# A new work order for a one-core attention and convolution kernel: sines first, fewer filter transfers

## The chip, the cores and the metric

The kernel runs on one core of one Trainium2 chip. The metric is the device time of one execution in microseconds (us). The kernel before took 321.59 us as the median of three runs (320.0, 321.59 and 323.23).

The engines, with the names that the profile gives them: PE is TensorE (matmuls; PEld its weight loads), DVE is VectorE, ACT is ScalarE, POOL is GpSimd, SP is SyncE, which here only issues DMAs. POOL issues DMAs too.

## What is computed

Two layers. The first is linear attention with exponential features, for 8 batches, 8 heads, 576 positions and heads of 64; the second is a gated convolution over the 576 positions, with a circular convolution that the reference does by an FFT:

```python
def phi(x):
    proj = np.einsum('bhsd,df->bhsf', x, w_phi)
    proj = proj - np.max(np.abs(proj), axis=-1, keepdims=True)
    return np.concatenate([np.exp(proj), np.exp(-proj)], axis=-1)
q_p, k_p = (phi(q), phi(k))
kv = np.einsum('bhsf,bhsd->bhfd', k_p, v)
z = np.sum(k_p, axis=2)
num = np.einsum('bhsf,bhfd->bhsd', q_p, kv)
den = np.einsum('bhsf,bhf->bhs', q_p, z)[..., None] + 1e-06
x = (num / den).transpose(0, 2, 1, 3).reshape(8, 576, 512)
...
proj = x @ w_proj
x1, x2, x3 = proj[..., :D], proj[..., D:2 * D], proj[..., 2 * D:]
X2 = np.fft.rfft(x2, n=S, axis=1)
H = np.fft.rfft(filter_fft, n=S, axis=0)[None, :, :]
y = x1 * np.fft.irfft(X2 * H, n=S, axis=1) * x3
return y @ w_out
```

Inputs and output are float32; the kernel multiplies in bfloat16 and accumulates in float32. w_phi is 64 by 128, w_proj 512 by 1536, the filter 576 by 512, w_out 512 by 512, the output 8 by 576 by 512.

## The kernel before

The work is cut into steps, one small method each, and the order of all steps is written out by hand as one long string, `PLAN`. A word of it is a step with its arguments; DVE, ACT or POOL among the arguments picks the engine that does it, and `@n` picks the PSUM bank (of eight) where it starts. `run` reads the words one after the other and emits their instructions. So each engine, and each engine's own list of DMA issues, does its instructions in the order of the words; between engines only data and buffers decide, through semaphores. A step that waits holds up everything behind it on its engine.

The rows of `seq` are taken modulo 9, so that 576 positions are 64 groups of 9, and the two halves X (heads 0 to 3 and 4 to 7) are loaded together. b is the batch, v one of four pairs of heads (v of 0 and 1 in half X = 0, of 2 and 3 in X = 1), m one of four column blocks.

Steps that the change and the prediction touch:

- Loads: `loadh,k,0,X` and `loadh,q,0,X` (L581) load a half of batch 0, `load,n,b` (L575) a whole q, k or v, `w_load,proj,kt` (L565) a third of w_proj (the parts of x1, x2, x3), `w_load,out` w_out. POOL issues these, with a cast to bfloat16. `filt_load` (L496) and `filt_loadt` (L500) load the filter, SP issues these.
- Transposes: batch 0's q and k go through PE (`pt`, L597) and are copied out by `pte` (L286 or L284); from batch 1 on `trh,n,b,X` (L587) does it as a DMA transpose of half X, issued by SP. The attention's output x is transposed by `ptx` on PE in batch 0, with `ptxe` copying it out, and by `trx` and `trxt` as DMA transposes later.
- Tables of the convolution's transform: `gen_part`, `gen_ident`, `gen_rows`, `gen_back` on POOL, `gen_cols` and `gen_angles` on DVE, and `gen_sin` (L456, twelve sines in four calls) on ACT. `D1m` and `D1e` mirror one of them, `gen_five` (L477 to L490) copies the ends of some into M5, `gen_neg` and `gen_ends` make variants for the last batch. The filter is folded by `filt_fold` (L508) and transformed by five `H` (L526), emptied by `H_ev`.
- Attention: `Pk`, `Qn` (L616, L623) and their rests `Pkt`, `Qnt` are the projections, `maxk`, `maxq` (L692) their maxima, `ex`, `exkt`, `exqt` (L678, L681, L686) the exponentials, `em` those of the maxima. `mhi`, `mlo`, `trm`, `trme` bring q's maxima to the other side, `Pq` (L650) projects q once more with them taken off. `vs` scales v, `KV` (L754) and `KVe` make the sums, `NE` (L768), `rc`, `xn` the quotient.
- Convolution: `f1` (L836), `f2` (L842) fold x, `F` (L848, L852) transforms it, `Fe`, `Fet` empty it, `X1`, `X2`, `X3` (L892, L870) project, `X1e`, `tm` form the gate, `Y1` (L880) multiplies by the filter, `m3` (L884) adds two parts, `I` (L945) transforms back, `Ie`, `Ip`, `Im` and `ym` (L993) finish; batch 7 uses `J` (L983) and `yj` (L987) for this. `O` (L1004) is the last product, `Oe` empties it, `st` stores it (two DMAs of 128 KB each). `yt` moves a rest of yT.

ACT computes a sine or an exponential with a table that must be loaded when the function changes (ACT_TABLE_LOAD in the trace); copies need none. The compiler puts these loads in.

Some pairs of DVE and POOL steps are kept apart: `port` lets a POOL step of the kinds in `PORT` wait for the last such DVE step (or `gen_angles`, `yt`) before it in the string.

The loop that makes the program out of the string:

```python
for word in PLAN.split():
    name, _, bank = word.partition("@")
```

## Time and profile before

| | us |
|---|---|
| median of three runs | 321.59 |
| the profiled execution | 316.38 |
| its span, first to last instruction | 314.6 |
| PE busy | 275.2 (87%) |
| DVE busy | 263.1 (84%) |
| ACT busy | 220.8 (70%) |
| POOL busy | 215.6 (69%) |
| granted TensorE clock, mean | 0.991 |

The profile is of one execution. A window has its busy times for each engine; a group is a line with its operation, its tiles, the count and the duration of one; the chain of waits goes back from the last instruction to what released each step. "issue" in it is time in which an engine waited for nothing that the profile shows. A busy share of 100% doesn't mean that PE gives all that it could, since matmuls overlap and their ends are modelled. The larger DMA groups of the opening: sixteen filter transfers of 64 KB with a median of 5.3 us from issue to landing, k and q of a batch (576 KB) with 8.3 and 10.1 us, a third of w_proj (512 KB) with 17.9 us.

### The profile page before, as it was taken

To read this page: it belongs to the slowest core of one execution; us is meant where nothing else is said; L and a number is where in the kernel's file an instruction comes from. 1 tells how busy PE (TensorE), PEld (TensorE's weight loads), DVE (VectorE), ACT (ScalarE), POOL (GpSimd) and SP (SyncE) were. 2 spreads that over 40 slices of the span, in tenths; PEclk is the share of its full clock that TensorE was granted. 3 is DMA by queue.
4 is the path that set the end of the run, shared out by engine and by line. 5 is a ranking of instruction groups with operands and counts; after the bars stand their busy time and mean duration, and the time that the engine had idled before them with its cause. 6 is when DMAs were issued, how large, how long until landed. Compare 5 with 4: busy or idle time off the path is not lost.

```text
span 314.6 us, 10164 instructions
## 1 busy us (share of the span) xinstructions
PE 275.2 (87%) x4266; PEld 200.3 (64%) x4289; DVE 263.1 (84%) x466; ACT 220.8 (70%) x369; POOL 215.6 (69%) x183
## 2 busy tenths in 40 slices
PE   1366668999899999999998979999999999999981
PEld 1233357767687777687666747786678676867750
DVE  8498769999989999979996898989999968883940
...
GB/s 127 225 210 178 197 180 172 117 185 85 128 124 176 193 150 103 176 186 117 131 184 115 136 123 51 75 115 145 165 48 19 147 114 70 3 58 154 36 9 158
DMA packets 72030, 39.98 MB, mean 127 GB/s; under 512 B 52336, under 2 KB 66800, under 8 KB 71984
## 3 DMA queue, kind: packets, MB, share of 16 engines
...
## 4 chain that ended last, share of the span: by engine, by line
PE 69%; DVE 11%; issue 6%; DMA 5%; ACT 4%; POOL 2%; SPq 0%; ACTq 0%; DVEq 0%; POOLq 0%
PE ps L892 16%; PE ps L870 10%; PE ps L1004 9%; PE ps L754 5%; PE ps L945 5%; PE ps L768 4%; DVE mq L692 3%; PE ps L848 3%; PE ps L852 2%; DMA fl<-in_moe_filter_fft_dram 2%; DMA flt<-in_moe_filter_fft_dram 2%; PE ps L901 2%; PE ps L650 2%; PE ps L656 2%; PE ps L616 2%
## 5 line engine op out<-in xcount | busy, mean ns | idle before, releaser
L892 PE MATMUL ps<-xT,wproj 128*128 128x256 bf16 x512 | 63.4, 273 | 0.0
L892 PEld LDWEIGHTS <-wproj 128*128 128x128 bf16 x512 | 48.3, 98 | 8.7
L692 DVE TENSOR_REDUCE mq<-ps 128x8 f32<-128x1024 f32 (+1 forms) x40 | 43.6, 1110 | 3.4 <-PE ps L623 2.9
L993 POOL TENSOR_TENSOR yT<-cv,x1s 128x576 bf16<-128x576 f32 x28 | 35.3, 1279 | 15.8 <-DVE cv L952 12.7
L692 DVE TENSOR_REDUCE mk<-ps 128x8 f32<-128x1024 f32 (+1 forms) x40 | 44.0, 1109 | 0.1
L836 POOL TENSOR_TENSOR SD<-xn 128x512 bf16<-128x512 bf16 x25 | 28.4, 1153 | 21.6 <-DVE xn L787 18.1
L678 ACT ACTIVATE Eqp<-ps 128x1024 bf16<-128x1024 f32 x32 | 32.6, 1025 | 10.5 <-PE ps L656 8.9
L739 POOL TENSOR_TENSOR vm<-vn,vm 128x1152 bf16<-128x1152 bf16 x16 | 34.4, 2151 | 7.7 <-ACT vm L733 4.5
L678 ACT ACTIVATE Ekm<-ps 128x1024 bf16<-128x1024 f32 x32 | 32.7, 1029 | 6.4 <-DVE mk L692 3.7
L842 POOL TENSOR_TENSOR xf<-SD 128x512 bf16<-128x512 bf16 x30 | 34.0, 1153 | 3.4 <-DVE xf L842 1.9
L1004 PE MATMUL ps<-wout,yT 128*128 128x512 bf16 x134 | 33.6, 379 | 2.2 <-DVE yT L987 0.8
L739 POOL TENSOR_TENSOR vp<-vn,vp 128x1152 bf16<-128x1152 bf16 x16 | 34.4, 2150 | 1.6 <-ACT vp L733 1.6
L678 ACT ACTIVATE Eqm<-ps 128x1024 bf16<-128x1024 f32 x32 | 32.7, 1028 | 2.5 <-PE ps L656 2.4
L678 ACT ACTIVATE Ekp<-ps 128x1024 bf16<-128x1024 f32 x32 | 32.9, 1032 | 1.4 <-PE ps L616 1.3
L870 PE MATMUL ps<-wproj,XF 128*128 128x512 bf16 x119 | 29.9, 380 | 0.8 <-issue 0.5
L945 PE MATMUL ps<-inv,T 128*128 128x288 bf16 x168 | 23.2, 286 | 0.2 <-DVE mq L692 0.2
L952 DVE TENSOR_TENSOR cv<-es,ps 128x288 f32<-128x288 f32 x56 | 22.1, 445 | 1.5 <-ACT es L949 1.3
L949 ACT COPY es<-ps 128x288 f32<-128x288 f32 x28 | 11.0, 402 | 17.2 <-PE ps L945 17.2
L1004 PEld LDWEIGHTS <-yT 128*128 128x128 bf16 x144 | 13.1, 97 | 15.5 <-issue 2.0
L933 DVE TENSOR_TENSOR x1s<-ps,x1s 128x512 bf16<-128x512 f32 x32 | 21.5, 683 | 1.3 <-PE ps L892 1.0
L787 DVE TENSOR_TENSOR xn<-ps,r 128x512 bf16<-128x512 f32 x32 | 21.7, 685 | 0.8
L284 ACT CAST x1s<-ps 128x512 bf16<-128x512 f32 (+1 forms) x27 | 14.1, 533 | 11.1 <-PE ps L892 8.3
...
## 6 DMA issues: line engine op xcount, KB each, us to landing
...
qn<-in_q_dram POOLq DMA_DIRECT2D x7, 576.0 KB, 10.1
...
wproj<-in_moe_w_proj_dram POOLq DMA_DIRECT2D x3, 512.0 KB, 17.9
...
```

Source lines behind the costliest of these rows:

```text
L678: self.nc.scalar.activation(e, p, AF.Exp, bias=0.0, scale=1.0 if g == "p" else -1.0)
L692: self.nc.vector.tensor_reduce(out=out, in_=src, axis=AX.X, op=ALU.max, apply_absolute_value=True)
L739: self.eng(eng).tensor_tensor(out=t[:, :, :, 0:64], in0=self.at("vn", b)[:, 2 * X:2 * X + 2], in1=t[:, :, :, 64:65].to_broadcast([128, 2, ...
L787: self.nc.vector.tensor_tensor(out=o, in0=n[:, :, :, 0:64], in1=self.at("r", 4 * b + v).to_broadcast([128, 2, 4, 64]), op=ALU.mult)
L836: self.eng(eng).tensor_tensor(out=o[:, :, 2 * i:2 * i + 2, :], in0=x[:, :, 0:2, :], in1=x[:, :, 2:4, :], op=ALU.subtract if i else ALU.add)
L842: self.eng(eng).tensor_tensor(out=o[:, :, 2 * i:2 * i + 2, :], in0=x[:, :, 0:4:2, :], in1=x[:, :, 1:4:2, :], op=ALU.subtract if i else ALU ...
L870: self.mm(self.pb(0), l, w[:, kt, 512:1024], start=(kt == 0), stop=(kt == 3))
L892: self.mm(o[:, d], w[:, kt, f0 + 128 * m:f0 + 128 * m + 128], y[:, 1, ::-1, ::-1] if d else y[:, 0], start=(kt == 0), stop=(kt == 3))
L945: self.mm(self.pb(e, 0, 288), l, inv[:, 2 * e + i if i < 2 else 4 + e, :], start=(i == 0), stop=(i == 2))
L952: self.nc.vector.tensor_tensor(out=self.at("cv", 4 * b + m)[:, :, odd, :], in0=self.at("es", 4 * b + m).rearrange("p (x t) -> p x t", t=32 ...
L993: self.eng(eng).tensor_tensor(out=self.at("yT", b)[:, m, 0:SEQ], in0=self.at("cv", 4 * b + m).rearrange("p x h t -> p (x h t)"), in1=self. ...
L1004: self.mm(self.pb(0), y[:, kt, 128 * c:128 * c + 128], w[:, kt, :], start=(kt == 0), stop=(kt == 3))
```

## The change

The string `PLAN` is replaced by another with the same 1,454 steps. 116 of them go to another engine, and nearly all stand elsewhere. In the opening: the first loads are q's halves (X = 1 before X = 0), then k's; q and w_proj of batch 1 go ahead of v of batch 0; w_out is loaded after batch 0's `vs` and `gen_ends`. All four `gen_angles` come before the copies of the transposed q and k, and all four `gen_sin` before the first exponential. `gen_five` goes from DVE to POOL, behind the folds. q's two DMA transposes of batch 1 change places (X = 1 first), and `Qn,1,0` follows `Pq,0,0`. In the counts by engine: `f1` on DVE 7 to 1, `f2` on DVE 2 to 1, `m3` on DVE 8 to 3, `X1e` on DVE 13 to 6, `KVe` on DVE 3 to 6, `Oe` on DVE 8 to 14, `ptxe` and `ptxte` from DVE to ACT, `H_ev` on DVE 4 to 3, one `vs` from POOL to DVE. The second change is in `filt_load`: a call makes two transfers of 64 rows (128 KB) instead of four of 32 rows (64 KB), and fills the same places over the four calls.

```diff
--- before
+++ after
 PLAN = """
-w_load,phi filt_load,0 filt_load,2 filt_loadt filt_load,1 filt_load,3 gen_part loadh,k,0,0 gen_ident
-loadh,q,0,0 gen_rows,0 loadh,k,0,1 zeros gen_cols,0 gen_cols,1 gen_angles,0 w_phi gen_angles,2
-pt,k,0,0,1@0 pte,DVE,k,0,0,1@0 pt,k,0,0,0@1 pte,DVE,k,0,0,0@1 Pk,0,0@0 filt_fold,DVE,2 loadh,q,0,1
-load,v,0 load,q,1 w_load,out w_load,proj,1 gen_back gen_rows,1 maxk,0,0@0 Pk,0,1@2 pt,q,0,0,0@4
-gen_one pte,DVE,q,0,0,0@4 pt,k,0,1,1@5 pt,k,0,1,0@6 pte,DVE,k,0,1,0@6 pte,DVE,k,0,1,1@5 Pk,0,2@4
-pt,q,0,0,1@6 gen_angles,4 pte,DVE,q,0,0,1@6 gen_sin,0 gen_sin,2 ex,k,m,0,0@0 ex,k,p,0,2@4
-ex,k,m,0,2@4 ex,k,m,0,1@2 maxk,0,2@4 pt,q,0,1,1@7 pt,q,0,1,0@6 ex,k,p,0,0@0 pte,ACT,q,0,1,1@7 D1m@4
-D1e,ACT@4 pte,ACT,q,0,1,0@6 maxk,0,1@2 Pkt,0@0 maxkt,0@0 ex,k,p,0,1@2 gen_five,DVE em,p,0,0
-exkt,m,0@0 Pk,0,3@4 maxk,0,3@4 em,m,0,0 exkt,p,0@0 gen_sin,4 ex,k,m,0,3@4 Qnt,0@6 Qn,0,2@2
-maxq,0,2@2 maxqt,0@6 Qn,0,3@0 Qn,0,1@2 maxq,0,3@0 maxq,0,1@2 Qn,0,0@6 maxq,0,0@6 mhi,0 em,m,0,1
-em,p,0,1 ex,k,p,0,3@4 trh,q,1,0 trh,q,1,1 w_load,proj,0 load,k,1 trh,k,1,0 w_load,proj,2 load,k,2
-trh,k,1,1 trh,k,2,1 filt_fold,POOL,1 filt_fold,POOL,0 trh,k,2,0 vs,POOL,p,0,0 load,v,1 vs,POOL,m,0,0
-gen_ends,POOL mlo,POOL,0 H,1@0 H,0@1 H,3@2 H,4@3 trm,0@6 H,2@7 trme,ACT,0@6 Pq,0,1@4 H_ev,ACT,3@2
-H_ev,DVE,0@1 H_ev,DVE,1@0 H_ev,DVE,4@3 ex,q,p,0,1@4 ex,q,m,0,1@4 Qn,1,1@0 maxq,1,1@0 load,q,2
-vs,POOL,m,0,1 vs,POOL,p,0,1 Pq,0,0@2 Qn,1,0@0 H_ev,DVE,2@7 maxq,1,0@0 ex,q,p,0,0@2 Pqt,0@4
-exqt,p,0@4 exqt,m,0@4 KV,0,0@6 KVe,ACT,0,0@6 ex,q,m,0,0@2 gen_angles,3 KV,0,1@0 gen_sin,3
-KVe,DVE,0,1@0 NE,0,1@6 NE,0,0@2 NEt,0@0 rc,0,1@6 Pq,0,3@4 ex,q,m,0,3@4 ex,q,p,0,3@4 rc,0,0@2
-xn,0,0@2 rct,0@0 xnt,0,1@0 xn,0,1@6 ptx,0,0@2 ptxe,DVE,0,0@2 xnt,0,0@0 ptx,0,1@6 ptxe,DVE,0,1@6
-f1,POOL,0,0,1 f1,POOL,0,0,0 f2,POOL,0,0,1 f2,POOL,0,0,0 Qn,1,3@2 Qnt,1@0 maxq,1,3@2 maxqt,1@0
-Pq,0,2@6 ex,q,m,0,2@6 ex,q,p,0,2@6 ptxt,0@2 ptxte,DVE,0@2 Qn,1,2@4 maxq,1,2@4 NE,0,3@0 X1t,0@2
-X1te,ACT,0@2 gen_neg mhi,1 mlo,POOL,1 NE,0,2@6 rc,0,3@0 xn,0,3@0 rc,0,2@6 xn,0,2@6 f1,DVE,0,1,0
-f1,POOL,0,1,1 f2,POOL,0,1,1 f2,POOL,0,1,0 F,0,1@2 ptx,0,3@0 ptxe,DVE,0,3@0 Fe,ACT,0,1@2
-Fet,ACT,0,1@2 F,0,0@4 Fet,ACT,0,0@4 Pk,1,1@6 ptx,0,2@1 ptxe,DVE,0,2@1 ex,k,m,1,1@6 Fe,ACT,0,0@4
...
-Y1,7,2@4 m3,DVE,7,1 X1te,ACT,7@7 X1e,ACT,7,2@2 X3,7,2@1 X3,7,3@7 X3,7,1@0 X1e,ACT,7,3@5
-X1e,ACT,7,1@6 X3t,7@4 tm,7,2@1 tm,7,1@0 tm,7,3@7 J,7,3@5 tmt,7@4 J,7,0@0 yj,7,0@0 yj,7,3@5 J,7,2@3
-yj,7,2@3 J,7,1@0 yj,7,1@0 yt,ACT,7 O,7,2@0 Oe,ACT,7,2@0 O,7,3@1 st,7,2 Oe,ACT,7,3@1 st,7,3 O,7,1@3
-Oe,ACT,7,1@3 O,7,4@0 O,7,0@1 Oe,ACT,7,0@1 Oe,ACT,7,4@0 st,7,1 st,7,0 st,7,4
+gen_part gen_ident loadh,q,0,1 loadh,q,0,0 gen_rows,1 gen_rows,0 pt,q,0,0,0@0 pt,q,0,0,1@1
+loadh,k,0,0 loadh,k,0,1 pt,k,0,1,1@2 pt,k,0,1,0@3 load,q,1 w_load,proj,1 load,v,0 pt,q,0,1,1@4
+pt,q,0,1,0@5 w_load,phi filt_load,3 filt_load,0 filt_load,2 filt_loadt filt_load,1 zeros gen_cols,0
+gen_cols,1 w_phi gen_angles,3 gen_angles,2 gen_angles,0 gen_angles,4 pte,DVE,q,0,0,1@1
+pte,DVE,q,0,0,0@0 filt_fold,DVE,2 pt,k,0,0,1@6 pt,k,0,0,0@7 pte,DVE,q,0,1,1@4 pte,DVE,q,0,1,0@5
+pte,DVE,k,0,1,0@3 pte,DVE,k,0,0,0@7 Qn,0,2@4 Qnt,0@0 maxq,0,2@4 maxqt,0@0 gen_sin,2 gen_sin,3
+gen_sin,0 trh,q,1,1 trh,q,1,0 w_load,proj,0 load,k,1 w_load,proj,2 load,q,2 filt_fold,POOL,0
+gen_back gen_sin,4 pte,ACT,k,0,1,1@2 pte,ACT,k,0,0,1@6 Pkt,0@6 exkt,p,0@6 Qn,0,0@2 filt_fold,POOL,1
+trh,k,1,0 trh,k,1,1 maxq,0,0@2 exkt,m,0@6 maxkt,0@6 Pk,0,0@4 ex,k,p,0,0@4 maxk,0,0@4 Pk,0,1@0
+ex,k,m,0,1@0 D1m@2 D1e,ACT@2 maxk,0,1@0 gen_neg ex,k,m,0,0@4 Qn,0,3@6 maxq,0,3@6 Qn,0,1@2
+ex,k,p,0,1@0 em,m,0,0 maxq,0,1@2 Pk,0,2@4 ex,k,m,0,2@4 H,0@6 gen_one H_ev,DVE,0@6 mhi,0 Pk,0,3@0
+ex,k,m,0,3@0 em,p,0,0 ex,k,p,0,2@4 gen_five,POOL H,4@7 mlo,POOL,0 maxk,0,3@0 trm,0@2 H,1@3 H,3@6
+maxk,0,2@4 trme,DVE,0@2 H_ev,ACT,4@7 H_ev,DVE,1@3 ex,k,p,0,3@0 vs,POOL,m,0,0 vs,POOL,p,0,0 H,2@7
+Pq,0,0@4 em,p,0,1 H_ev,ACT,3@6 ex,q,p,0,0@4 ex,q,m,0,0@4 em,m,0,1 Qn,1,0@0 Pq,0,1@2 maxq,1,0@0
+ex,q,p,0,1@2 ex,q,m,0,1@2 H_ev,DVE,2@7 Qn,1,2@0 maxq,1,2@0 Qn,1,1@4 maxq,1,1@4 KV,0,0@6
+KVe,ACT,0,0@6 vs,POOL,p,0,1 vs,POOL,m,0,1 Pq,0,2@0 ex,q,m,0,2@0 ex,q,p,0,2@0 gen_ends,POOL Qn,1,3@2
+KV,0,1@6 KVe,ACT,0,1@6 maxq,1,3@2 Qnt,1@4 Pqt,0@2 maxqt,1@4 exqt,m,0@2 mhi,1 NE,0,0@0 rc,0,0@0
+mlo,DVE,1 xn,0,0@0 exqt,p,0@2 Pq,0,3@6 ex,q,p,0,3@6 ex,q,m,0,3@6 NE,0,1@4 rc,0,1@4 xn,0,1@4 NE,0,2@2
+rc,0,2@2 NEt,0@0 rct,0@0 xn,0,2@2 xnt,0,1@0 xnt,0,0@0 ptx,0,0@4 trm,1@5 ptxe,ACT,0,0@4 NE,0,3@6
+rc,0,3@6 xn,0,3@6 ptx,0,1@2 trme,ACT,1@5 ptxe,ACT,0,1@2 ptx,0,2@4 ptxe,ACT,0,2@4 trh,q,2,0 Qn,2,0@0
+maxq,2,0@0 trh,q,2,1 Pk,1,1@2 ptxt,0@7 Qn,2,2@4 ptx,0,3@6 ex,k,p,1,1@2 ptxte,ACT,0@7 maxq,2,2@4
+w_load,out load,v,1 load,k,2 Qn,2,3@0 maxq,2,3@0 f1,POOL,0,0,1 f1,POOL,0,0,0 f1,POOL,0,1,1
+f1,POOL,0,1,0 f2,POOL,0,0,1 f2,POOL,0,1,1 f2,POOL,0,1,0 f2,POOL,0,0,0 load,q,3 X1t,0@7
+ptxe,ACT,0,3@6 ex,k,m,1,1@2 X1te,ACT,0@7 Pkt,1@4 exkt,m,1@4 exkt,p,1@4 X1,0,2@6 maxk,1,1@2 maxkt,1@4
+X1e,ACT,0,2@6 X1,0,0@7 Qn,2,1@0 maxq,2,1@0 Pk,1,0@2 Qnt,2@4 maxqt,2@4 X1e,ACT,0,0@7 ex,k,p,1,0@2
+F,0,3@6 Fet,DVE,0,3@6 Fe,DVE,0,3@6 ex,k,m,1,0@2 F,0,2@0 mhi,2 Fet,ACT,0,2@0 Fe,ACT,0,2@0 F,0,0@4
+Fet,ACT,0,0@4 maxk,1,0@2 mlo,POOL,2 load,v,2 load,k,3 Fe,DVE,0,0@4 Pk,1,3@6 ex,k,m,1,3@6 X3,0,2@0
...
+X2,7,3@0 m3,POOL,7,0 X3,7,3@4 X3,7,1@6 X2,7,4@7 Y1,7,2@1 Y1,7,3@0 X1t,7@0 Y1,7,4@7 tm,7,2@5 O,6,1@1
+X1,7,1@7 X1e,DVE,7,1@7 O,6,0@5 tm,7,3@4 Oe,ACT,6,0@5 O,6,3@2 X3,7,0@4 tm,7,1@6 Oe,DVE,6,1@1
+m3,POOL,7,1 X1te,ACT,7@0 J,7,1@6 J,7,0@0 tmt,7@3 tm,7,0@4 yj,7,0@0 yj,7,1@6 J,7,3@4 yj,7,3@4
+Oe,ACT,6,3@2 J,7,2@0 yj,7,2@0 yt,DVE,7 O,6,2@6 Oe,ACT,6,2@6 st,6,1 st,6,0 st,6,3 st,6,2 O,7,1@0
+O,7,2@6 Oe,DVE,7,2@6 O,7,4@1 Oe,DVE,7,4@1 O,7,3@5 Oe,DVE,7,3@5 Oe,ACT,7,1@0 O,7,0@6 Oe,ACT,7,0@6
+st,7,1 st,7,2 st,7,4 st,7,3 st,7,0
 """
...
     def filt_load(self, a):
-        base = 288 * (a // 2) + 5 * (a % 2)
-        for i in range(4):
-            self.nc.sync.dma_start(out=self.fl[32 * i:32 * i + 32, a, :],
-                                   in_=self.dram["filt"][base + i:base + i + 280:9, :])
+        src = self.dram["filt"].rearrange("(h t j) f -> h t j f", h=2, j=9)[a // 2]
+        for i in (2 * (a % 2), 2 * (a % 2) + 1):
+            self.nc.sync.dma_start(out=self.fl[32 * i:32 * i + 32, a - a % 2:a - a % 2 + 2, :],
+                                   in_=src[:, i:i + 6:5, :])
```

257 lines of the change are left out of this document (126 added, 131 removed).

## The prediction, made before any run

> **What bounds the kernel now.** I read the table by stage first, then the chain of waits, the ScalarE timeline, the SyncE timeline, the groups by line, and the tail. The table by stage has the window, its length, and for each engine busy time and instructions, then the granted clock, the DMA share and GB/s:
>
> ```profile
> 0.00:58.00 58.00, 34.13 (x521) 24.03 (x523) 45.75 (x118) 40.15 (x64) 36.90 (x51) 0.97 1.15 181
> 58.00:290.00 232.00, 223.95 (x3624) 165.25 (x3643) 205.65 (x334) 175.81 (x297) 178.73 (x134) 1.00 0.72 119
> 290.00:314.60 24.60, 17.16 (x125) 11.03 (x124) 11.67 (x15) 4.82 (x10) 0.00 (x0) 0.95 0.34 73
> ```
>
> There are three stages. In the middle one PE is busy 97% of the time and VectorE 89%, with GpSimd at 77%: PE sets the pace and VectorE, which empties its banks, is close behind. In the opening 58 us PE is busy for only 34, and what is missing there can be won. A busy PE is not yet a PE at its pace: taking each matmul's median distance from start to start times its count, the whole program needs 253 us of PE, of which 28.4 are done at 58.4 us of the span and 225 remain. The chain of waits (start, length, what) tells what the opening hangs on:
>
> ```profile
> 23.86 4.66 POOL fe L508 x2
> ...
> 42.69 2.84 issue
> ...
> 47.19 1.28 ACT L678
> ```
>
> The folds of the filter, a wait that the profile can't name, and the exponentials' table. ScalarE's timeline around the second set of sines, and the start of the third:
>
> ```profile
> 24.93 1.28 ACT L456 ACT_TABLE_LOAD   x1
> 26.23 2.00 ACT L456 ACTIVATE inv<-turn,cols 128x288 bf16<-128x288 f32 x4
> 28.24 1.28 ACT L678 ACT_TABLE_LOAD   x1
> ...
> 41.91 1.28 ACT L456 ACT_TABLE_LOAD   x1
> ```
>
> Sines come in three sets, so tables are loaded six times; the sixth, at 47.19, comes after 3.03 us in which ScalarE had nothing to do, because the row that it waits for stood behind PE's 2.84. Batch 0's last exponential ends at 52.27. SyncE's timeline shows the filter and the first DMA transposes:
>
> ```profile
> 1.98 3.83 SPq L496 DMA_DIRECT2D fl<-in_moe_filter_fft_dram  x8
> 6.15 0.47 SPq L500 DMA_DIRECT2D flt<-in_moe_filter_fft_dram  x1
> 6.67 7.19 SPq L496 DMA_DIRECT2D fl<-in_moe_filter_fft_dram  x8
> 21.05 10.64 SPq L587 DMA_TRANSPOSE qT<-qn  x2
> 34.53 17.99 SPq L587 DMA_TRANSPOSE kT<-kn  x4
> ```
>
> Batch 1's q lands at 21.03; its two transposes start then and land at 34.53 and 42.47.
>
> **The change part by part. Sines.** Two pairs of table loads go: 4 x 1.28 = 5.1 us of ScalarE. The 12 sines stay, but all stand before the first exponential, and so do their angles on VectorE. That moves the start back: angles cost about 0.86 + 0.82 for each of two pieces with 576 columns and 0.42 + 0.52 for each of five with 288, 8.3 us with a first row of 1.05 for 0.86; columns end at 4.7, so the angles end at 13.2, and only then VectorE copies out the transposed q and k. Two of the eight copies are ScalarE's, after its last sine (some 14.3). PE's transposes wait for the fourth half load: in the trace the first four land at 5.8, 10.2, 12.8 and 14.9. Copies of 0.45 end at 16.6 to 18.4; with one product and the table load of 1.28 the first exponential comes at 18.8 to 20.6 (take 19.7), against 15.14 now.
>
> From there ScalarE has a queue without tables. By the distances of back-to-back rows, the steps up to batch 0's first pair for q are ten large exponentials at 0.91, two smaller at 0.49, D1's eviction 0.70, the negation 0.6, three H evictions at 0.5, and five tiny steps (exponentials of the maxima, a cast) at 0.12: 13.5 us, to 33.2. The rest of batch 0 (six large, two small, two evictions of KV at 0.47, one cast) is 7.5 us: 40.7, if nothing is late, 11.6 us before today's 52.27.
>
> **A new wait.** Something is late. PE has Qn,1,0 directly behind Pq,0,0, and it needs the second transpose of q's batch 1, since the order of the two is swapped. q of batch 1 is now the fifth load, where v lies today (18.33); GpSimd starts 0.6 us later because the identity comes first, so 18.7. The transposes share the DMA engines with the loads: between 32 and 42 us the packet records have about 143 packets of 256 B and 144 of loads in each us, and a transpose has 1,152 such packets, 8 us; the first needs 3.4 us from issue to its first packet. So they land at some 30 and 38 to 40. The loads queued behind (six of 512 packets) last until then, so nothing frees the engines earlier. Behind Qn,1,0 on PE stand Pq,0,1 and both KV; ScalarE, done at 33.2, waits for Pq,0,1. From 38.5 the chain Qn, Pq and 7.5 us, plus 0.6 of small waits, ends at 47.2 (46.2 to 48.7).
>
> What is late next is VectorE and then GpSimd: four maxima of q, NE's reciprocals and products, four maxima for batch 2, and GpSimd's f1 and f2 (seven times 1.15 before F,0,3). F,0,3 comes at about 57. In PE's own pace that matmul stands at 28.4, which today is reached at 58.4: 1.4 us won. VectorE by then has done 49 us of its work where today it has done 45.7, of which a part counts later. I take **2.0 us won in the opening**, between 7 (no wait for the transpose) and -2 (it lands at 42.5, as the second does today).
>
> **Filter.** Eight issues fewer at 0.42 us save 3.4 us of SyncE, whose next step, the transpose, waits for q anyway: nothing. The bytes are the same. The folds start today at 23.86, 5.3 us after the last filter landing (18.5), because GpSimd's order holds them behind VectorE's gen_five. The change puts them first and gen_five on GpSimd (0.38 + 6 x 0.18 on VectorE; no row on GpSimd; between 1.3 and, by the ratio 2.7 of f1's rows on both engines below, 3.6; take 2.5). So the cover is gone: a filter landing 1 us later moves the folds by 1 us. H,0 and H,4 follow at some 25, still before trm, which waits for the maxima until 28.5. I cost it at nothing, 2 us at worst.
>
> **Middle stage.** VectorE gives away, net, six f1 (3.0), one f2 (0.4), five m3 (3.4) and seven X1 evictions (4.8), and gets six Oe (4.1), three KVe (2.1), one vs (no row there; 0.7 to 1.2 by m3's row, whose size is nearest; 1.2) and small ones (0.3): 3.9 less. The opening takes 4.0 more from it (five copies of x, gen_five, one H eviction). GpSimd gets 6.9 + 1.2 + 10.6 for f1, f2, m3, loses a vs of 2.15, and has gen_five: 19 more on 216. The rows of both engines for the two moved kinds (minimum, median, maximum in ns):
>
> ```profile
> L836 POOL TENSOR_TENSOR SD<-xn x25: 1142/1155/1159, 47.6 to 283.1; 128x512 bf16<-128x512 bf16 x25
> L836 DVE TENSOR_TENSOR SD<-xn x7: 411/424/981, 54.1 to 279.8; 128x512 bf16<-128x512 bf16 x7
> ...
> L884 POOL TENSOR_TENSOR T<-T,T x8: 2107/2122/2134, 66.9 to 203.0; 128x1024 bf16<-128x1024 bf16 x8
> L884 DVE TENSOR_TENSOR T<-T,T x8: 642/684/693, 138.2 to 296.7; 128x1024 bf16<-128x1024 bf16 x8
> ```
>
> GpSimd goes to about 84% of the stage, VectorE to 87%. PE loses about 23 us against its pace there, and the longer gaps that the trace ends with a name are VectorE's (0.46 to 0.65 each). VectorE's relief is worth up to 3.9, and 1 more if its lead from the opening counts; if the moved steps all show their longer time it costs 5 x 1.44 + 6 x 0.73 + 0.73 = 12.3. Nearest is the row of the stage itself, PE waiting for VectorE: **2 us won**, from 5 won to 8 lost (two thirds of 12.3).
>
> **Tail.** PE's timeline at the end (start, length, what, and the idle time before it with its releaser):
>
> ```profile
> 303.58 4.48 PE L1004 MATMUL ps<-wout,yT 128*128 128x512 bf16 x19 [0.85 <-DVE yT L987]
> ```
>
> PE waits 0.85 us for VectorE's last yT before the last products; the change puts O,6,2 (four matmuls at 0.216) into that gap. The stores cost SyncE 1.28 us each as today, one more now stands before batch 7's five. **0.5 won**, 1.3 to -0.8.
>
> Sum: 2.0 + 2.0 + 0.5 = 4.5. The profiled execution took 316.38 (span 314.6 and 1.8 around it): 311.9. The runs' median, 321.59, is 5.2 above it: 317.1, which I give as 317.
>
> **Two rules of the Trainium skill.** The row 24.93 is followed by its sine at 26.23: a load costs 1.28 here and nothing after it. ScalarE: Activation LUTs (What ACT_TABLE_LOAD costs) adds a drain and gives 2.66 for a switch; by it the four removed would be an estimated 10.6 of ScalarE instead of 5.1. The trace does not show the drain, so the row stands.
>
> GPSIMD Engine Reference (Key points) says that GpSimd shares its SBUF interfaces with VectorE and contends with its instructions of two SBUF inputs. By that rule more GpSimd work slows both. The GpSimd rows spread by under 2%, so the trace hardly bears it out; one VectorE row of 981 against 424 may be such a meeting.
>
> **The rivals.** *GpSimd becomes the late one (slower).* F waits for f2 and I for m3 in the middle stage, and VectorE's relief buys nothing. For it: 12.3 us of added time, GpSimd in order with vs of 2.15 between. Against: 16% of its stage stays idle. It decides where PE's gaps before L848 or L945 name GpSimd; 8 lost, less 2.5 won elsewhere: 327. Chance 0.21.
>
> *Contention of the two engines.* Each of 13 moved steps met by a VectorE step costs at most 0.56 (981 - 424): 7.2, less 4.5: 324. Chance 0.03.
>
> *No wait for the transpose.* It lands before 32; the opening wins 7, the sum 9.5: 312. For it: PE's order puts it there. Against: both landings of today. Chance 0.13.
>
> *The opening gives nothing.* The transpose lands at 42.5 or the filter is late by 2: opening -2 and the rest 2.5 won: 321. Also here: code for PE comes late again, as in the 2.84 of "issue" at 42.69. Chance 0.17.
>
> *The change doesn't do what it says.* Each engine runs its list in order, so nothing undoes it: 0.01.
>
> **How the numbers follow.** The forecast has 0.45 and its own range is 313 to 321. About 1% (3.2 us) can be told from no change. Faster, below 318.4: 0.38 of the forecast and 0.13 without the wait, 0.51. Slower, above 324.8: GpSimd 0.19, contention 0.01 and 0.02 of the opening's case, 0.22. Within: the rest, 0.27. The range 310 to 326 leaves out the lower part of the case without the wait and half of the GpSimd case.
>
> **What would show it.** Two table loads, the second at 17 to 20; ScalarE's first exponential near 19.7; a gap of 4 to 7 us on PE before L623 that a transpose of q ends at 38 to 40; batch 0's last exponential at 46 to 49; VectorE's busy time near 255 (263 - 7.9) and GpSimd's near 234; PE gaps in the middle stage named VectorE. Wrong, if PE passes Qn,1,0 before 34 or after 42, if gaps before L848 and L945 name GpSimd, or if the tail after the last J is longer than now.

## The result, and the profile after

The changed kernel took 324.08 us (median of 20 runs, 321.59 to 326.7), the kernel before beside it 320.72 (20 runs, 316.31 to 323.68): a ratio of 1.0147, 95% interval 1.0112 to 1.0182. It is slower, by 1.5% by the ratio; the two medians alone are 3.4 us apart, 1.0%. The forecast was 317, faster, and its range 310 to 326 holds the time.

All runs, each beside the kernel before on the same chip (medians in us). The ratio leaves out runs over 1.5% above the kernel's fastest; in e11_all these are four of six and in e12_filt8 six of twelve, so for those two the medians are read.

| run | what it is | time | before | ratio, 95% interval |
|---|---|---|---|---|
| after | the change | 324.08 | 320.72 | 1.0147, 1.0112 to 1.0182 |
| c_after | the change again | 323.98 | 320.45 | 1.0120, 1.0051 to 1.0188 |
| e1_qn_later | opening: Qn of batch 1 later | 323.83 | 320.56 | 1.0127, 1.0083 to 1.0170 |
| e2_loads_later | middle: four loads later | 320.29 | 320.56 | 1.0006, 0.9968 to 1.0043 |
| e3_sp_order | middle: two transposes earlier on SP | 322.17 | 320.56 | 1.0085, 1.0045 to 1.0126 |
| e4_filt16 | filter in sixteen again | 322.11 | 320.56 | 1.0062, 1.0028 to 1.0096 |
| e5_sines | before, with all sines first | 328.97 | 320.45 | 1.0288, 1.0232 to 1.0344 |
| e6_dve | moved steps back on DVE | 335.39 | 321.34 | 1.0461, 1.0393 to 1.0529 |
| e8_open2 | e1 and three loads later | 332.09 | 320.45 | 1.0377, 1.0322 to 1.0432 |
| e9_warm | PE kept busy in three waits | 322.00 | 320.45 | 1.0080, 1.0040 to 1.0120 |
| e10_open3 | e8 with the loads placed otherwise | 333.78 | 321.34 | 1.0430, 1.0365 to 1.0495 |
| e11_all | e10, middle's edits, sixteen | 322.06 | 321.34 | 0.9871, 0.9775 to 0.9967 |
| e12_filt8 | before, filter in eight | 321.05 | 321.34 | 0.9948, 0.9896 to 1.0000 |
| e13_k2_early | e11 with one load back in place | 310.53 | 320.27 | 0.9745, 0.9700 to 0.9789 |
| e14_middle | only the middle's edits | 316.17 | 320.27 | 0.9900, 0.9867 to 0.9932 |
| e15_filt8 | e13 with eight transfers | 311.97 | 320.27 | 0.9796, 0.9745 to 0.9847 |
| e16_opening | only the opening's edits | 319.68 | 320.68 | 0.9983, 0.9945 to 1.0021 |
| e17_warm | e13, PE kept busy in two waits | 308.52 | 320.68 | 0.9631, 0.9589 to 0.9674 |

The table by stage of the changed kernel's profile (columns as before; its profiled execution took 324.05, span 322.3):

```profile
0.00:58.00 58.00, 29.58 (x507) 22.49 (x508) 41.66 (x104) 35.54 (x61) 35.35 (x54) 0.85 1.14 181
58.00:290.00 232.00, 222.20 (x3591) 163.27 (x3590) 199.84 (x319) 175.54 (x298) 190.87 (x144) 0.99 0.72 117
290.00:322.30 32.30, 25.24 (x196) 16.51 (x193) 17.16 (x25) 4.44 (x9) 7.11 (x5) 0.96 0.35 76
```

In the opening PE is busy 4.55 us less than before (29.58 against 34.13), in the middle stage 1.75 less, though there every other engine but GpSimd has less to do. Busy time is not work done, since a matmul at half pace is busy for longer; the work is compared below, with one common pace. The changed kernel's chain of waits (start, length, what):

```profile
19.99 19.43 DMA qT<-qn
...
46.65 2.21 issue
...
116.18 2.38 DMA xTt<-xnt
...
152.94 9.00 DMA qT<-qn
...
283.69 4.52 DMA xT<-xn
```

Where before the folds, unnamed waits and a table stood, four DMA transposes stand now; DMA has 15% of the span in this chain, against 5% before. On PE's timeline three of them end a gap of 3 us or more (the last bracket is the idle time before and its releaser); the fourth, x's at 283.69, ends one of 0.59:

```profile
39.47 0.61 PE L624 MATMUL ps<-wphi,qT 64*128 64x128 bf16 x8 [6.96 <-DMA qT<-qn]
...
118.60 1.04 PE L902 MATMUL ps<-xTt,wproj 128*128 128x64 bf16 x16 [3.22 <-DMA xTt<-xnt]
...
161.99 0.40 PE L624 MATMUL ps<-wphi,qT 64*128 64x128 bf16 x8 [3.65 <-DMA qT<-qn]
```

The first was forecast. The other two were not: the middle stage before had no gap that a DMA ended. The trace of the second set of runs, c_after, has the same three gaps (5.67 us at 38.5, 3.14 at 118.6, 4.13 at 162.8).

What stands ahead of the transpose that ends the gap at 118.60 is shown by two timelines. GpSimd's has three loads of 576 KB:

```profile
101.85 0.80 POOL L576 DMA_DIRECT2D vn<-in_v_dram  x1
102.64 0.75 POOL L576 DMA_DIRECT2D kn<-in_k_dram  x1
103.37 0.76 POOL L576 DMA_DIRECT2D qn<-in_q_dram  x1
```

SyncE's has the transposes:

```profile
104.43 8.22 SPq L588 DMA_TRANSPOSE qT<-qn  x2
112.74 3.38 SPq L807 DMA_TRANSPOSE xT<-xn  x1
116.18 1.25 SPq L812 DMA_TRANSPOSE xTt<-xnt  x1
```

q's two transposes of batch 4, behind the loads, hold SyncE for 8.22 us and land 12.4 and 10.4 us after their issue. So xTt is issued only at 116.18; it then takes 2.38. Before the other gap, GpSimd issued a load of k at 152.61, and q's transpose of batch 5, issued at 152.94, took 9.00.

A gap can also cost more than its length, because PE works at half pace when it comes out. Windows of the same profile (granted clock third from the end):

```profile
32.60:36.20 3.60, 0.00 (x0) 0.00 (x0) 1.02 (x2) 2.21 (x4) 2.92 (x2) 1.00 1.20 196
36.30:43.00 6.70, 2.99 (x62) 2.70 (x64) 2.71 (x3) 1.94 (x2) 4.36 (x6) 0.50 1.31 174
118.20:121.50 3.30, 2.90 (x43) 2.49 (x44) 1.28 (x2) 1.82 (x3) 0.00 (x0) 0.50 0.67 130
162.60:165.90 3.30, 3.30 (x27) 1.95 (x23) 1.56 (x2) 2.52 (x4) 0.93 (x2) 0.50 0.50 111
```

In this trace a stretch of 3.41 us at half clock goes with each of the waits of 2.21, 3.22 and 3.65 us, starting between 0.5 us before and 1.1 us behind the wait's end, and one of 6.83 us (36.2 to 43.1) with the wait of 6.96. In the middle stage before there was no such stretch. The Trainium skill (TensorE: Matmul & The Clock Gate, Part 1) says that a free-running window of about 3.4 us decides, that an idle one halves the clock and a busy one restores it. The lengths, 3.41 and 6.83 us, agree. But no wholly idle window was needed here: a wait of 2.21 us was enough, and so was sparse work without a gap over 0.9 us ahead of 22.6. Taking each trace of this case in windows of 3.41 us, on the grid of its clock records, the clock after a window at full clock in which PE was busy under 40% was half in all 42 cases, between 40% and 60% in 28 of 51, and above 60% in none.

With one common pace for both traces (median distance of each kind of matmul, times its count), PE has done 25.3 us of its work at 60 us against 27.6 before, 61.2 against 62.7 at 100, 74.6 against 80.9 at 120, 101.7 against 107.7 at 150 and 115.6 against 126.0 at 170: it loses about 2 us in the opening, wins one back, and loses 5 and 4 around the two waits. Of 10.4 at 170 it wins some back later; at the end the spans differ by 7.7, more than the medians, because the trace of before is of one of its fastest runs. (The trace of before has 23 matmul records fewer, so the late values understate its lead.)

### The profile page after: what moved, and what is told of

Its sections match the earlier page's. It is cut to its first block, busy times and chain, and to the rows that moved or that the text cites. A ratio compares the mean times of both kernels' runs of the same rounds, so it can differ in the third digit from the quotient of the medians.

```text
span 322.3 us, 10183 instructions
## 1 busy us (share of the span) xinstructions
PE 277.0 (86%) x4289; PEld 202.3 (63%) x4289; DVE 258.7 (80%) x446; ACT 215.5 (67%) x367; POOL 233.3 (72%) x201
## 3 DMA queue, kind: packets, MB, share of 16 engines
q1 hardware_dynamic: 57040, 23.08, 43.1%
HBM read 33.75 MB, written 9.44 MB: 134 GB/s over the span
## 4 chain that ended last, share of the span: by engine, by line
PE 70%; DMA 15%; DVE 7%; issue 3%; POOL 2%; SPq 1%; ACT 1%; DVEq 0%; POOLq 0%
PE ps L893 16%; PE ps L871 11%; DMA qT<-qn 9%; PE ps L1005 9%; PE ps L769 5%; PE ps L755 5%; PE ps L946 5%; DMA qn<-in_q_dram 4%; PE ps L651 3%; DVE mq L693 2%; PE ps L902 2%; PE ps L849 2%; PE ps L624 2%; PE ps L617 2%; PE ps L657 2%
## 5 line engine op out<-in xcount | busy, mean ns | idle before, releaser
L893 PE MATMUL ps<-xT,wproj 128*128 128x256 bf16 x512 | 65.9, 277 | 0.6 <-DMA xT<-xn 0.6
L837 POOL TENSOR_TENSOR SD<-xn 128x512 bf16<-128x512 bf16 x31 | 35.2, 1152 | 21.5 <-DVE xn L788 17.8
L740 POOL TENSOR_TENSOR vp<-vn,vp 128x1152 bf16<-128x1152 bf16 x15 | 32.2, 2150 | 11.8 <-DVE T L885 8.1
L1005 PE MATMUL ps<-wout,yT 128*128 128x512 bf16 x144 | 34.9, 380 | 0.0
L885 POOL TENSOR_TENSOR T<-T,T 128x1024 bf16<-128x1024 bf16 x13 | 27.6, 2122 | 8.7 <-DVE T L881 5.3
L871 PE MATMUL ps<-wproj,XF 128*128 128x512 bf16 x128 | 31.7, 380 | 0.0
L285 ACT COPY o<-ps 128x512 f32<-128x512 f32 x22 | 12.8, 593 | 28.0 <-PE ps L1005 27.2
L285 ACT CAST x1s<-ps 128x512 bf16<-128x512 f32 (+1 forms) x33 | 17.9, 554 | 12.2 <-PE ps L893 5.0
L624 PE MATMUL ps<-wphi,qT 64*128 64x128 bf16 x256 | 14.0, 239 | 12.6 <-DMA qT<-qn 10.6
L769 PE MATMUL ps<-KVs,Eqm 128*128 128x65 bf16 x256 | 20.7, 198 | 3.2 <-issue 3.2
```

The costliest lines, as they stand in the source:

```text
L285: self.nc.scalar.copy(dst, src)
L740: self.eng(eng).tensor_tensor(out=t[:, :, :, 0:64], in0=self.at("vn", b)[:, 2 * X:2 * X + 2], in1=t[:, :, :, 64:65].to_broadcast([128, 2, ...
L769: self.mm(self.pb(u, 65 * a, 65 * a + 65), E, KVs[:, u, v, s, :], start=(s == 0), stop=(s == 1))
L837: self.eng(eng).tensor_tensor(out=o[:, :, 2 * i:2 * i + 2, :], in0=x[:, :, 0:2, :], in1=x[:, :, 2:4, :], op=ALU.subtract if i else ALU.add)
L871: self.mm(self.pb(0), l, w[:, kt, 512:1024], start=(kt == 0), stop=(kt == 3))
L893: self.mm(o[:, d], w[:, kt, f0 + 128 * m:f0 + 128 * m + 128], y[:, 1, ::-1, ::-1] if d else y[:, 0], start=(kt == 0), stop=(kt == 3))
```

## The experiments

**The opening's wait.** In the changed order PE has `Qn,1,0` in front of batch 0's work. The first edit moves it:

```diff
-Qn,1,0@0 Pq,0,1@2 maxq,1,0@0 ex,q,p,0,1@2 ... KV,0,0@6 ... Pq,0,2@0 ... KV,0,1@6 ... Pq,0,3@6
+Pq,0,1@2 ex,q,p,0,1@2 ... KV,0,0@6 ... Pq,0,2@0 ... KV,0,1@6 ... Pq,0,3@4 ... Qn,1,0@0 maxq,1,0@0
```

> The changed order, with batch 1's Qn and their maxima put behind batch 0's Pq and KV on PE, VectorE and ScalarE. Theory A (in the opening the new order stands still because PE's Qn,1,0 waits for q's second transpose with batch 0's Pq and KV behind it): the gap of 6.96 us before L624 near 39.4 falls under 3, batch 0's last exponential comes at 42 to 46 instead of 52.1, and 3 to 6 us of the 324.1 go: 318 to 321, ratio to the kernel before about 0.997. Rival B (PE would have lost that time anyhow, to late code and to the lower granted clock): the last exponential comes earlier but F,0,3 does not, and the time stays within 1.5 us of 324.1, ratio 1.010 to 1.019.

Measured 323.83: nothing. The wait at 39 went, batch 0's last exponential ended at 42.3 instead of 52.1, and by the common pace PE was 3.7 us ahead of the changed kernel at 40 us. At 60 us 0.4 of it was left. Three timelines of this run show where it went (start, length, what). GpSimd's, with three loads:

```profile
38.44 0.84 POOL L569 DMA_DIRECT2D wout<-in_moe_w_out_dram  x1
39.28 0.75 POOL L576 DMA_DIRECT2D vn<-in_v_dram  x1
40.01 0.76 POOL L576 DMA_DIRECT2D kn<-in_k_dram  x1
```

SyncE's, with the pair of transposes issued among them:

```profile
38.73 10.89 SPq L588 DMA_TRANSPOSE qT<-qn  x2
```

And PE's, where it next waits:

```profile
53.48 0.40 PE L624 MATMUL ps<-wphi,qT 64*128 64x128 bf16 x8 [3.23 <-DMA qT<-qn]
```

q's transposes of batch 2 were issued among three loads (1.7 MB) and landed 14.7 us later. So the next run put the loads off:

```diff
-w_load,out load,v,1 load,k,2 Qn,2,3@0 maxq,2,3@0 f1,POOL,0,0,1 f1,POOL,0,0,0 ... load,q,3 ... load,k,3
+Qn,2,3@0 maxq,2,3@0 f1,POOL,0,0,1 f1,POOL,0,0,0 load,v,1 ... load,k,2 load,q,3 ... load,k,3 w_load,out
```

> The first experiment (batch 1's Qn behind batch 0's Pq and KV) and, with it, three loads (w_out, v of batch 1, k of batch 2) issued later by GpSimd, behind its first steps of f1 and f2. Theory A (in the first experiment q's transposes of batch 2 were slow, 14.7 us from issue to landing, because these loads were issued just ahead): they land by 46 to 48 instead of 53.4, the gap of 3.23 before L624 goes, the lead of 3.8 us of PE work at 40 us is kept, and 4 to 6 us go against the first experiment's 323.8: 318 to 320, ratio 0.992 to 0.998. Rival B (PE would have lost the time anyhow): the gap goes but others take its place, and the time stays within 1.5 us of 323.8.

Measured 332.09, 8 us slower. The mechanism held: the same transposes, issued at 38.73 again, landed after 4.2 us, and PE was 2.7 us ahead of the changed kernel at 60. But the loads now came together, and k of batch 2 came late. GpSimd's timeline of this run:

```profile
57.98 0.79 POOL L575 DMA_DIRECT2D kn<-in_k_dram  x1
58.76 0.75 POOL L575 DMA_DIRECT2D qn<-in_q_dram  x1
...
59.73 0.79 POOL L575 DMA_DIRECT2D vn<-in_v_dram  x1
60.51 0.75 POOL L575 DMA_DIRECT2D kn<-in_k_dram  x1
61.24 0.76 POOL L568 DMA_DIRECT2D wout<-in_moe_w_out_dram  x1
```

PE's, with the two gaps that followed:

```profile
77.44 0.23 PE L631 MATMUL ps<-wphi,kT 64*128 64x128 bf16 x2 [3.90 <-DMA kT<-kn]
83.43 0.29 PE L631 MATMUL ps<-wphi,kT 64*128 64x128 bf16 x2 [5.76 <-DMA kT<-kn]
```

k's transposes, issued at 63.85 and 66.32 behind five loads, took 13.5 and 17.1 us. A third placing has all three loads behind the first two f1:

> As the experiment with the three loads put off, but all three (v of 1, k of 2, w_out) issued together behind GpSimd's first two f1, so that none comes behind the others' burst at 58 to 61. Theory A: q's transposes of batch 2 land at 43 to 45, those of k of batch 2 by 68, no gap over 2 us between 43 and 100, PE's work done at 60 and 70 us is 3 us ahead of the changed kernel's and stays so; 3 to 5 us faster than its 324: 319 to 321, ratio 0.996 to 1.003. Rival B (PE would have lost the time anyhow): other gaps take their place, within 1.5 us of 324.

Measured 333.78: q's transposes landed by 44.7 as expected, but k's of batch 2, issued at 59.5 and 61.8 with three loads between 58.9 and 61.5, at 75.1 and 81.6; three gaps of 3 us followed between 69 and 86, one ended by these transposes, two without a name (issue).

**The middle stage's waits.** Two edits, each alone. First GpSimd's loads, then SyncE's order:

```diff
-load,v,3 load,k,5 load,q,5 ... mlo,POOL,3 ... ym,POOL,1,1 ... load,k,6 ... f2,POOL,3,1,1
+mlo,POOL,3 load,v,3 ... ym,POOL,1,1 load,q,5 load,k,5 ... f2,POOL,3,1,1 load,k,6
```

> The changed order, with four loads (v of batch 3, k and q of 5, k of 6) issued 12 to 25 us and 4 us later by GpSimd; SyncE's order is untouched. Theory A (the waits of 3.22 at 118.6 and 3.65 at 162 are transposes slowed by loads that were issued just ahead of them): q's transposes of batch 4 take 3 to 4 us from issue to landing instead of 12.4 and 10.4, both gaps fall under 1, and 4 to 7 us go: 317 to 320, ratio about 0.994. Rival C (SyncE's order alone makes them late): both gaps stay at 3 or more and the time stays within 1.5 us of 324.1.

```diff
-st,0,2 trh,q,4,0 trh,q,4,1 trx,2,1 trxt,1 ... trh,q,5,1 st,0,3 trx,3,1 ... trh,q,5,0
+st,0,2 trxt,1 trh,q,4,0 trh,q,4,1 trx,2,1 ... trh,q,5,1 trh,q,5,0 st,0,3 trx,3,1 ...
```

> The changed order, with two words moved on SyncE's queue: trxt,1 ahead of q's two transposes of batch 4, and the second transpose of q of batch 5 directly behind the first; the loads are untouched. Rival C (SyncE's order alone): both gaps go, 6 to 7 us, 317 to 318, ratio 0.992. Theory A (loads just ahead): the gap at 162 goes, since the transpose is now issued ahead of the load, but at 118 PE only waits for q's second transpose of batch 4 instead, so that gap keeps 1.5 to 3 us; 3.5 to 5 go: 319 to 320.5, ratio 0.999.

The loads gave 3.7 us (320.29), the order 1.8 (322.17). With the loads put off, q's transposes of batch 4 took 3.2 and 4.8 us from issue to landing instead of 12.4 and 10.4; both gaps went, and one of 3.31 came at 122.3 (a transpose of x just behind v's load), and two of 0.90 and 1.64 at 166 and 168 (GpSimd's `vs`, held up behind `load,k,7`, which waits for a transpose). In the other run the gaps at 118 and 162 went too, and smaller ones came, the largest 2.25 at 159.6. Neither "loads alone" nor "order alone" survives: PE waits for a transpose that has a load just ahead of it, and either can be moved. The run with both, with `load,k,6` put off further and `load,k,7` behind its `vs` (v of batch 3 stays early):

> The changed order and its filter, with only the edits of the middle stage: trxt of batch 1 and q's second transpose of batch 5 earlier on SyncE, and four loads put off on GpSimd (k and q of 5, k of 6, k of 7). The opening is untouched. Theory A: both gaps of 3 to 4 us (118 and 162) and the half clock behind them go and nothing over 1.5 us takes their place: 7 to 9 off 324: 315 to 317, ratio 0.982 to 0.989. Rival I (the waits move on): one gap of 2 us or more stays between 100 and 190 and the time is that of the edits tried singly, 320 to 322, ratio 0.998 to 1.005.

Measured 316.17, in the expected place, 7.9 below the change and 1.0% faster than before. SyncE's timeline of that run has q's transposes of batches 4 and 5:

```profile
104.23 3.58 SPq L587 DMA_TRANSPOSE qT<-qn  x2
...
140.91 3.63 SPq L587 DMA_TRANSPOSE qT<-qn  x2
```

Batch 4's pair, with one load still under way ahead of it (v's) instead of three, landed 4.6 and 4.2 us after issue instead of 12.4 and 10.4, and held SyncE for 3.58 us instead of 8.22. Batch 5's, with no load ahead, took 3.8 and 3.4. No gap over 0.73 us is left on PE between 103 and 290.

A late transpose is not always a loss. In this run an xTt issued at 164.57 still took 9.2 us, and in the kernel before one of q's, issued at 103.36, took 7.0 and one of k's, issued at 122.62 among loads, 14.3. None of them ends a gap of PE: its order needed them later.

**GpSimd, the rival of the forecast.** Fifteen steps of f1, f2 and m3 go back to VectorE, at their places in the new order (`m3,POOL,5,1` to `m3,DVE,5,1` and so on):

> The changed order with 15 steps of f1, f2 and m3 that it moved to GpSimd put back on VectorE (19 us less on GpSimd, 7 more on VectorE). The rival of the forecast (GpSimd is the late one in the middle stage): 3 to 8 us faster, 316 to 321. Theory A (the middle stage's losses are waits for transposes, no engine's work): within 1.5 us of 324, ratio 1.010 to 1.018, with both gaps of 3 to 4 us still there.

Measured 335.39. GpSimd was not the late one. With the steps back at these places VectorE became it: from 58 us to the end, PE's gaps of 0.15 us or more that VectorE ends add up to 5.5 us (one is 2.42 at 291), against 0.3 in the changed kernel and 4.4 before. The two waits of 3 us stayed. So the relief of VectorE that was forecast did come; what ate it up is that the gaps which a DMA ends went from none before to 7.5 us. The 11 us are the price of these steps in the new order only. Theory A's "within 1.5 us" fell as well: the engines have no slack for 7 us more on VectorE.

**The filter.** The old `filt_load` in the new order, then the new one in the old:

> The changed order with the filter loaded as before, in sixteen transfers. The forecast's step (the filter part costs and brings nothing): within 1 us of 324.1, ratio 1.012 to 1.018; the last filter landing moves from 14.2 to about 18 and the folds, at 18.6 and 21.8 now, start at most 1 us later. Rival D (the folds have lost their cover, so a later filter moves everything behind it): the folds and H come 2 to 4 us later and the time is 1 to 3 us longer, ratio 1.018 to 1.024.

> The kernel before with one part of the change alone: the filter in eight transfers of 64 rows. The forecast's step (nothing): within 1 us of the kernel before, ratio 0.997 to 1.003. Theory H (the larger transfers are issued in half the time and come ahead of the q and k halves in the DMA engines): the third and fourth half land 1 to 2.5 us later than 12.8 and 14.9, the filter's last part 3 to 4 earlier than 18.5, and the time is 1 to 2.5 us longer, ratio 1.003 to 1.008.

The first gave 2 us (322.11), the second nothing (321.05 against 321.34). PE's timeline at the start of the run with sixteen transfers in the new order:

```profile
8.68 1.14 PE L598 MATMUL ps<-ident,qn 128*128 128x128 bf16 x9 [8.68 <-DMA qn<-in_q_dram]
12.87 1.14 PE L598 MATMUL ps<-ident,kn 128*128 128x128 bf16 x9 [3.05 <-DMA kn<-in_k_dram]
```

The same lines of the changed kernel, with eight:

```profile
9.89 1.14 PE L598 MATMUL ps<-ident,qn 128*128 128x128 bf16 x9 [9.89 <-DMA qn<-in_q_dram]
15.44 1.14 PE L598 MATMUL ps<-ident,kn 128*128 128x128 bf16 x9 [4.40 <-DMA kn<-in_k_dram]
```

The halves that PE waits for land 1.2 and 2.6 us earlier with sixteen. In the order of before, eight transfers hold the halves up as well. PE's timeline of e12_filt8:

```profile
12.71 0.71 PE L597 MATMUL ps<-ident,qn 128*128 128x128 bf16 x5 [2.78 <-DMA qn<-in_q_dram]
15.00 1.14 PE L597 MATMUL ps<-ident,kn 128*128 128x128 bf16 x9 [1.57 <-DMA kn<-in_k_dram]
```

The same lines of the kernel before, with sixteen:

```profile
10.26 0.72 PE L597 MATMUL ps<-ident,qn 128*128 128x128 bf16 x5
12.88 1.14 PE L597 MATMUL ps<-ident,kn 128*128 128x128 bf16 x9 [1.91 <-DMA kn<-in_k_dram]
```

There the second, third and fourth half land 2.5, 2.1 and 1.1 us later with eight, but only 0.3 of it is left at the first H (28.86 against 28.56), where PE waits for GpSimd's folds in both traces. So the delay is the same kind in both orders, and it reaches the end only in the new one. Why the larger transfers hold the halves up, these runs don't tell.

**The sines alone.** The order of before, with `gen_angles,3`, `gen_sin,3` and `gen_sin,4` moved up to the other sines:

```diff
-pt,q,0,0,1@6 gen_angles,4 ... gen_sin,0 gen_sin,2 ex,k,m,0,0@0 ... gen_sin,4 ... gen_angles,3 ... gen_sin,3
+pt,q,0,0,1@6 gen_angles,4 gen_angles,3 ... gen_sin,0 gen_sin,2 gen_sin,3 gen_sin,4 ex,k,m,0,0@0 ...
```

> The order of before with one part of the change alone: all sines, and the angles they need, ahead of the first exponential. Four table loads of 1.28 us go. Theory A (ScalarE's time in the opening is not what the end waits for, since PE waits for transposes and late code): batch 0's last exponential comes up to 3 us earlier, but the time stays within 1.5 us of the kernel before, ratio 0.995 to 1.005. Rival E (the tables are on the path): 3 to 5 us faster, ratio 0.984 to 0.991.

Measured 328.97; both theories fell. ScalarE's timeline:

```profile
20.45 0.54 ACT L456 ACTIVATE inv<-turn,cols 128x288 bf16<-128x288 f32 x1 [10.03 <-DVE turn L435]
...
25.08 1.02 ACT L678 ACTIVATE Ekm<-ps 128x1024 bf16<-128x1024 f32 x1
```

The table loads went, but the sines now wait for angles that stand behind VectorE's copies, and the first exponential comes at 25.08 instead of 15.14. Sines first are only worth having with the angles first, as the change has them (first exponential at 20.4).

**The clock.** PE is given products of zeros in its waits:

```diff
+warm,28@0
 Qn,1,0@0
...
+warm,13@3
 X1t,1@3
...
+warm,15@0
 Qn,5,1@0
```

> The changed kernel with PE kept at work in three of its waits: 28, 13 and 15 products of zeros (128x512 each, 0.216 us) ahead of Qn,1,0, X1t,1 and Qn,5,1, which nothing reads; the waits themselves stay. Theory F (a wait costs more than its own length, because the granted clock falls to half after it): the half-clock stretches that begin at 36.2, 118.2 and 162.5 go, PE works them off at full pace and 3 to 5 us go, 319 to 321, ratio 0.999 to 1.003. Rival G (the clock's price is hidden by the other engines, which hold PE anyway): the stretches go, the time stays within 1 us of 324.1, ratio 1.011 to 1.018.

Measured 322.00, 2.0 less than the change beside it, with the waits still there. The windows of this run:

```profile
36.30:43.00 6.70, 5.75 (x130) 3.79 (x130) 3.34 (x4) 2.06 (x3) 4.80 (x6) 1.00 1.19 159
118.20:121.50 3.30, 3.30 (x47) 2.56 (x43) 1.66 (x3) 2.22 (x3) 0.94 (x1) 0.64 0.98 115
162.60:165.90 3.30, 3.30 (x40) 2.69 (x39) 1.97 (x3) 3.20 (x8) 0.26 (x1) 1.00 0.20 44
```

Of the three half-clock stretches that the products aimed at, those at 36 and 162 are gone, and one stays at 119.1, where a wait of 1.75 is left. The half clock does cost time, but less than expected. Another wait, of 3.27, came at 47.87, where the profile names no releaser ("issue"). Such a wait is called late code here: over the traces of all nineteen kernels and runs, each of the 41 waits of PE of 0.59 us or more that is called issue ends 1.25 to 1.63 us after a packet of 16 KB on the DMA queue that the profile calls instruction, which has 33 such packets in an execution. Of PE's 103 other waits of that length after 30 us, six do.

**All together.** The edits of e10, those of e14 for the middle stage and the sixteen transfers:

> All edits that removed a wait, together: the filter in sixteen transfers, Qn of batch 1 behind Pq and KV of batch 0, the three early loads put off as in the run beside it, trxt of batch 1 and q's second transpose of batch 5 earlier on SyncE, and four later loads put off. Theory A (waits for transposes behind loads, and the half clock that follows each, are what the change lost): their sum, 2 + 4 + 5 us and some 2 lost to what is late next, so 9 off 324: 313 to 317, ratio 0.977 to 0.990. If the waits only move, as in the earlier runs with one edit each: 319 to 322, ratio 0.995 to 1.004.

Its six runs spread from 314.95 to 326.13, median 322.06. Its trace, of a run of 323.32, has one long gap: 9.44 us at 82.5, for k's transposes of batch 2, issued at 60.26 and landed at 82.44 behind three loads, and 10.2 us of half clock, from 75.7 on, in and behind it. One load back in its old place:

```diff
-f1,POOL,0,0,0 load,v,1 load,k,2 w_load,out
+load,k,2 ... f1,POOL,0,0,0 load,v,1 w_load,out
```

> The run with all edits together, with one load back in its place of the change: k of batch 2 is issued at 38 to 39 again, ahead of the other two put off. Theory A (in that run the gap of 9.44 us at 82.5, and the 10.2 us of half clock behind it, come from k's transposes of batch 2, which wait behind three other loads because k itself came late): k's transposes of batch 2 land before 66, the gap goes, and 8 to 13 of its 322.1 go: 309 to 314, ratio 0.962 to 0.977. Rival I (the transposes only change places: what is let through first makes another late): a new gap of 3 us or more appears before 100 and the time stays at 318 to 322, ratio 0.990 to 1.002.

Measured 310.53, 2.5% faster than before (interval 2.1 to 3.0). The table by stage:

```profile
0.00:58.00 58.00, 35.61 (x567) 26.05 (x569) 46.48 (x111) 40.57 (x71) 40.30 (x59) 0.88 1.10 181
58.00:290.00 232.00, 225.79 (x3618) 167.48 (x3649) 203.73 (x324) 171.54 (x291) 192.93 (x143) 1.00 0.72 117
290.00:308.60 18.60, 11.74 (x75) 7.13 (x73) 7.56 (x13) 3.07 (x6) 0.00 (x0) 0.90 0.60 128
```

PE is busy 6.0 us more in the opening than in the changed kernel and 3.6 more in the middle stage; by the common pace it has done 29.2 us of its work at 60 us, against 25.3 there and 27.6 before. Then the parts of this version, taken back one at a time:

> As the run with k of batch 2 early, but with the changed kernel's eight filter transfers. Theory H (the eight come ahead of the q and k halves and hold up the whole opening): the third and fourth half land 1 to 2 us later and the time is 1 to 2.5 us over that run. Rival (the opening waits for q's transposes of batch 1, which come at 39 either way, so the filter's part is hidden): within 0.8 us of that run.

> The changed order and its filter, with only the edits of the opening: Qn of batch 1 behind Pq and KV of batch 0, and v of batch 1 and w_out put off behind GpSimd's first two f1. The middle stage is untouched. Theory A (the waits of the opening and of the middle stage are separate and add up): the run with both sets and eight transfers took 312.0, the one with the middle's alone 316.2, so the opening's edits are worth 4.2: 319 to 321 here, ratio 0.996 to 1.002, with both gaps of 3 to 4 us still there. Rival J (an earlier opening only waits longer at 118 and 162): those gaps grow by 2 us or more in sum and the time is 322.5 to 324.5.

Eight transfers cost 1.4 us here (311.97). The opening's edits alone took 319.68, 4.4 below the change's 324.08; with the middle's 7.9 that makes 12.3, and both together with the same filter are 12.1 below it. So the two stages' losses add up, within the noise of medians from different chips (about 1 us). Last, the fastest order with products of zeros in two waits of the opening (`warm,12@2` ahead of `pt,k,0,1,1`, `warm,8@0` ahead of `Qn,1,0`):

> The fastest run so far (all edits, k of batch 2 early), with PE kept at work in two waits of the opening: 12 products of zeros ahead of k's first transposes and 8 ahead of Qn,1,0, which nothing reads. Theory F (half-clock stretches cost time): the two of 6.83 us at 21.7 and 42.2 go or halve, and 1 to 3 of 310.5 go: 307.5 to 309.5. Rival G (in the opening the clock's price is hidden): the stretches go, the time stays within 0.8 us of 310.5.

Measured 308.52, 2.0 less. The half pace of the start ended earlier (first clock record, to full, at 14.4 instead of 18.2), the half-clock stretch at 45 is 3.41 us instead of 6.83, and the one in the twenties stayed. The late code moved too (the gap of 1.52 at 105 is gone), so the 2.0 are not shown to be the clock's alone.

## Why the prediction was wrong

**Right.** Two table loads, the second at 19.1 (17 to 20 forecast); the first exponential at 20.4 (19.7); the gap before L624 of 6.96 us ended by q's transpose at 39.4 (4 to 7 at 38 to 40); GpSimd's busy time 233.3 (234). GpSimd was not the bound, and no gap of PE in the middle stage names it. The rival that came nearest in time, contention of the two engines at 324, has no row for it: GpSimd's f1 takes 1152 ns on average, as before (1153).

**Signs that failed.** VectorE's busy time was 258.7, 4.4 less than before, where 255 and 7.9 less were forecast. Batch 0's last exponential ended at 52.1, not at 46 to 49. The longer gaps of PE in the middle stage name DMA, not VectorE. And the tail behind the last J, which was to be no longer than before, is longer by 0.5, though only because four matmuls moved into it.

**The opening, forecast 2.0 won.** The wait was where and as long as forecast; its price was mis-sized. The working let Qn, Pq and the exponentials take 8.7 us from 38.5 to 47.2. They took 12.6, from 39.47 to 52.09: behind `Qn,1,0`, three more Qn and their maxima stand ahead of the last Pq, PE worked at half clock to 43.1, and a wait of 2.21 us for late code, which the forecast had put in a rival, came at 46.65 (the kernel before has one of 2.84 in its opening). The two transposes landed at 31.8 and 39.4, near the forecast (30 and 38 to 40). The first F came at 60.7, not 57. At 60 us PE was 2.3 us behind instead of ahead, just outside the end of the term's range, 2 lost. `Qn,1,0` moved alone gave nothing (e1_qn_later); with v of batch 1 and w_out put off as well it gave 4.4 us against the change (e16_opening). By the common pace PE is then 0.8 us ahead of before at 60 us, and 1.6 with the sixteen filter transfers too (e13_k2_early): near the term, but only with other places for the loads. Two small slips of the working change nothing: in the trace of before the first packet of q's transpose came 3.9 us after its issue, not 3.4, and columns that end at 4.7 with 8.3 us of angles make 13.0, not 13.2.

**The middle stage, forecast 2.0 won.** This is the step that failed. Its term was worked out from the engines' busy time, with the danger in GpSimd, and it put PE's waits for transposes at nothing without a reason. The relief came (PE's gaps that VectorE ends fell from 4.4 us to 0.3), yet the stage lost: two waits for DMA transposes, 3.22 and 3.65 us, and a half clock behind each. The forecast had worked out in the opening that a transpose shares the DMA engines with the loads ahead of it, and did not ask in the middle stage which loads GpSimd would now issue just ahead of SyncE's transposes (three at 101.9 to 104.1, with q's transposes at 104.4). e14_middle measures what these waits cost: 7.9 us. That the stated range still holds the time is luck, because none of the cases that it was made of has these waits.

**The filter, forecast at nothing, 2 at worst.** It costs 1.4 to 2.0 us in the new order (e15_filt8, e4_filt16), so the outer end of the term holds, but by another way than the folds': it makes q's and k's halves later.

**The tail, forecast 0.5 won.** The wait of 0.85 before the last products is gone, as forecast. From the start of the last J to the end it is 17.42 us against 16.94, with four more matmuls (0.86) in it: about 0.4 won.

**The base.** The profile of before that the sum was made against (316.38) is nearly the fastest of that kernel's runs. The traces of e12_filt8, which has its order, and e5_sines, which nearly has it, show 4.2 and 4.0 us of late code before a NE at 172 to 185 and 6.83 us of half clock with it; the profile of before has 1.59 there and no half clock. The new order has no such wait there.
